# Loads of queries, keys and values from the fifth tile on issued by ScalarE instead of SyncE

## The chip, the cores and the metric

The kernel runs on one NeuronCore of a Trainium2 chip. The metric is the device time of one execution in microseconds (us). The engines are TensorE (PE in the profile; PEld is its loading of weights), VectorE (DVE), ScalarE (ACT), GpSimd (POOL) and SyncE (SP), which here only issues DMAs.

## The reference

Windowed causal attention over 8 batches of 8 heads, 576 positions and 64 columns a head, then one block of a network on the 4608 tokens of 512 columns:

```python
scores = scale * np.matmul(q, k.transpose(0, 1, 3, 2))
mask = (rel >= 0) & (rel < 64)                 # rel: query position less key position
attn = softmax(np.where(mask, scores, -1e9))
x = (attn @ v), heads side by side             # [4608, 512]
h = x @ w_in                                   # [4608, 1024]
solu = h * softmax(h)
ln = (solu - mean) / sqrt(var + 1e-6) * g_ln
out = ln @ w_out                               # [4608, 512]
```

All inputs and the output are float32.

## The kernel before

The 4608 tokens are 36 tiles of 128. One tile goes through these steps, each a function of the kernel:

- `load`: one DMA brings the tile's queries and keys (qk, 640 KB), one the values (v, 512 KB). Each has three buffers, so the load of a tile needs the matmuls of the tile three before it to be done: the scores for qk, `values` for v.
- `scores` and `softmax`: 32 small matmuls (L373) write pS; VectorE takes each head's row maximum (L388, nmx), ScalarE the exponentials (L393, sS and their sums sm), VectorE the reciprocals (L406, L409, rec), and GpSimd scales each head (L411).
- `cross` and `transposes`: the probabilities are transposed. From tile 5 on this is done by DMA: ScalarE copies four heads, split into 16-bit halves, into `raw` (L425), SyncE issues a transposing DMA inside SBUF (L428), and VectorE puts the halves together (L435, PT). Two such rounds make a tile.
- `values`: 32 matmuls (L470) into pO; ScalarE rounds them to xH (L484) and VectorE takes the rest xL (L485).
- `moe_in`: 24 matmuls (L513) into pH, of which there is one buffer, in two halves of 12.
- `moe_norm`: VectorE's maximum over pH (L528), ScalarE's exponential (L530, e), VectorE's product with pH (L533), which is pH's last reader, ScalarE's sum of squares (L539, sq), some short steps (mst), and GpSimd's scaling of e in two halves (L550).
- `moe_cross` and `moe_join`: e is transposed as the probabilities are: VectorE's copy into `raw` (L576), a transposing DMA (L579), VectorE's copy out of it (L589, y), then yH (ScalarE, L593) and yL (VectorE, L595). The first three and the last two tiles use TensorE instead (`moe_transpose`: L610, then yH at L619 and yL at L621).
- `moe_out`: 24 matmuls (L646) into pO, ScalarE's copy to ot (L653), and the store (L654).

Two passes of the weights are split into a rounded part and a rest, hence three matmuls for each pair of blocks. The first tiles use plain float32 matmuls (L502, L634) while the weights (`weight_block`, eight of them through SyncE and `raw`) are still prepared.

The main loop at the end of the kernel calls these functions tile by tile; from tile 6 on (`PAIRS`) two tiles form a group: `group(t)` does the values of tiles t+1 and t+2, the scores, softmax and `cross` of t+3 and t+4, and loads for later tiles. Nothing is issued there. Each call records operations in a `Plan`, with an engine, a cost in ns, what they read and write, and a latency. `Plan.order` then works out due times backwards from TensorE's order and lists all operations by a greedy simulation with those costs; the engines' queues stand in that order and run strictly in it. An operation marked `loose` (all of SyncE's from tile 4 on; `SPL = 3`) may be listed out of the order in which the loop made it. The keys in square brackets are the reads and writes by which the plan orders operations:

```python
plan.dma(P * P * 40, lambda: nc.sync.dma_start(QK(t), qk[t]), [], [("qk", t)],
         t > SPL)
self.op("SP", max(350, size // 340), emit, reads, writes, 2600, loose)
```

Of the kernel before, what the change touches and what calls it, by code (L numbers as in the profile page):

```python
# [18 lines left out]
P = 128  # L19
# [23 lines left out]
PAIRS = 6  # L43

SPL = 3

# [8 lines left out]
class Plan:  # L57
# [12 lines left out]
        self.ops.append((engine, cost, emit, reads, writes, lat + self.LATENCY, loose))  # L70

    def dma(self, size, emit, reads, writes, loose=False):
        self.op("SP", max(350, size // 340), emit, reads, writes, 2600, loose)

    def edges(self):

# [91 lines left out]
def tile_window_attention_solu_moe(  # L168
# [154 lines left out]
    def QK(t):  # L323
        return T("qk", t, [P, NPAIR * (2 * P + WIN)])
# [7 lines left out]
    def V(t, half):  # L332
        return T("v", t, [P, 2, DM])[:, half]

    def load(t, parts=range(2)):

        if 0 in parts:
            plan.dma(P * P * 40, lambda: nc.sync.dma_start(QK(t), qk[t]), [], [("qk", t)],
                     t > SPL)


        if 1 in parts:
            plan.dma(P * P * 32, lambda: nc.sync.dma_start(
                T("v", t, [P, 2, DM]).rearrange("p a n -> p (a n)"), v[t]), [], [("v", t)], t > SPL)

    def SS(t):
        return T("sS", t, [P, H, P])
# [73 lines left out]
    def cross(t):  # L421
        if t < CROSS_P:
            return
        for x in range(2):
            plan.op("ACT", 1050, lambda x=x: nc.scalar.copy(  # L425
                XP(t)[:, x], SS(t)[:, 4 * x:4 * x + 4].bitcast(U16).rearrange("p h (n w) -> p w (h n)", w=2)),
                [("sS", t, 4 * x + i) for i in range(4)], [("raw", NW + 2 * t, x)])
            plan.op("SP", 1250, lambda x=x: nc.sync.dma_start_transpose(  # L428
                XP(t)[:, 2 + x].rearrange("p w (h n) -> p (w h) n", h=4), XP(t)[:, x].rearrange("p w n -> p (w n)")),
                [("raw", NW + 2 * t, x)], [("raw", NW + 2 * t, 2 + x)], 2600, t > SPL)  # L430

# [164 lines left out]
                YL(t)[:, hs], Y(h), YH(t)[:, hs].bitcast(F32)),  # L596
                [("y", t, h), ("yH", t, h)], [("yL", t, h)])

    def moe_transpose(t):
        if crosses(t):  # L600
            moe_join(t)
            return
        for h in range(2):
            def pT(h=h):
                return PE_T(t, h)

            def emit(h=h, pT=pT):
                for f in range(4):
                    c = 4 * h + f
                    nc.tensor.transpose(pT()[:, f], E(t)[:, c * P:(c + 1) * P], ident)  # L610

            hs = slice(4 * h, 4 * h + 4)
            plan.op("PE", 430, emit, [("e", t, h)], [("pS", NTILE + t, h)])
            if t < PLAIN_OUT:
                plan.op("DVE", 620, lambda hs=hs, pT=pT: nc.vector.tensor_tensor(
                    YH(t)[:, hs], pT(), g_sb[:, hs].unsqueeze(2).to_broadcast([P, 4, P]), op=ALU.mult),
                    [("pS", NTILE + t, h), ("g",)], [("yH", t, h)])
                continue
            plan.op("ACT", 560, lambda hs=hs, pT=pT: nc.scalar.copy(YH(t)[:, hs], pT()),  # L619
                    [("pS", NTILE + t, h)], [("yH", t, h)])  # L620
            plan.op("DVE", 620, lambda hs=hs, pT=pT: nc.vector.tensor_sub(  # L621
                YL(t)[:, hs], pT(), YH(t)[:, hs].bitcast(F32)),
                [("pS", NTILE + t, h), ("yH", t, h)], [("yL", t, h)])

    def moe_out(t, middle=None):

        tag = ("pO", t)

        def PO():
            return T(*tag, [P, DM], pool=ps_o)  # L630

        if t < PLAIN_OUT:
            for f in range(NF):
                plan.op("PE", 860, lambda f=f: nc.tensor.matmul(  # L634
                    PO(), YH(t)[:, f], W32(NC + f // 2)[:, f % 2],
                    start=(f == 0), stop=(f == NF - 1)),
                    [("yH", t, f // 4), ("w", NC + f // 2), ("w", NC + f // 2, f % 2)], [tag])
        for f in range(NF if t >= PLAIN_OUT else 0):
            if f == NF // 2 and middle is not None:
                moe_transpose(middle)  # L640
            i, x = NC + f // 2, f % 2
            for k, (y, w, keys) in enumerate((
                    (YH, lambda i, x: WH(i, x), [("yH", t, f // 4), ("H", i, x)]),
                    (YH, lambda i, x: WL(i)[:, x], [("yH", t, f // 4), ("w", NW + i, x)]),
                    (YL, lambda i, x: WH(i, x), [("yL", t, f // 4), ("H", i, x)]))):
                plan.op("PE", 233, lambda f=f, i=i, x=x, k=k, y=y, w=w: nc.tensor.matmul(  # L646
                    PO(), y(t)[:, f], w(i, x), start=(f == k == 0), stop=(f == NF - 1 and k == 2)),
                    keys, [tag])

        def ot():  # L650
            return T("ot", t, [P, DM])

        plan.op("ACT", 580, lambda: nc.scalar.copy(ot(), PO()), [tag], [("ot", t)])  # L653
        plan.dma(P * DM * 4, lambda: nc.sync.dma_start(out[t * P:(t + 1) * P, :], ot()), [("ot", t)], [],  # L654
                 t > SPL)

# [30 lines left out]
    def group(t):  # L687
        on(values, t + 1)
        if t != PAIRS:
            on(values, t + 2)  # L690
        both = t + AHEAD, t + AHEAD + 1
        for u in both:
            on(scores, u)
        for u in (t + AHEAD + 2, t + AHEAD + 3):
            on(load, u, range(1))
        for u in (t + AHEAD + 1, t + AHEAD + 2):
            if u != PAIRS + AHEAD + 2:
                on(load, u, range(1, 2))
        for u in both:
            on(softmax, u)  # L700
            on(cross, u)

    for t in range(NTILE + BEHIND):
        if t < PAIRS:
            on(load, t + AHEAD + 1)
        if t == PAIRS - 1:
            on(load, t + AHEAD + 2, range(1))
        if t == PLAIN_IN:
# [6 lines left out]
        if t < BEHIND:  # L715
            on(moe_in, t, 1)
            on(moe_norm, t)
            on(moe_cross, t)
            on(transposes, t + 1)
            attend(t)  # L720
            on(values, t + 1)
        else:
            even = (t - PAIRS) % 2 == 0
            if t <= PAIRS + 1:
                on(transposes, t + 1)
            elif even:
                on(transposes, t + 1)
                on(transposes, t + 2)
            on(moe_in, t, 1)
            on(moe_norm, t)  # L730
            on(moe_cross, t)
            if t < NTILE:
                on(moe_transpose, t - BEHIND)
            if t < PAIRS:
                on(values, t + 1)
                attend(t)
            elif t == PAIRS + 1:
                on(values, t + 1)
                on(load, t + AHEAD + 1, range(1, 2))
            elif even:  # L740
                group(t)
            if t - BEHIND == PLAIN_OUT:
                for i in range(NC, NC + NF // 2):
                    split(i)

            last = NTILE - 1 <= t < NTILE + BEHIND - 1
            on(moe_out, t - BEHIND, *([t - BEHIND + 1] if last else []))
# [48 lines left out]
```

## Time and profile before

| | us |
|---|---|
| median of three runs | 534.41 (532.65 to 535.96) |
| the profiled execution | 536.71 |
| its span in the profile | 534.9 |
| PE / DVE / ACT / POOL busy | 508.7 / 419.2 / 357.2 / 221.6 |

All rows quoted below come from the profiled execution; their times count from the start of its span. A line of the chain or of the timeline has the start, the length, the engine, the source line and the tiles written and read (`pO<-PT,v`); in square brackets stands how long the engine was idle before and what ended that. SPq is SyncE's queue of DMA issues: a row's length there is the time of issuing, not of the transfer. A row of stretches gives the length, the busy time of each engine with its count, the granted clock of TensorE, the busy share of the DMA engines, and GB/s.

### The profile page before, as it was taken

What the parts mean: (1) busy time and instruction counts of PE and PEld (TensorE: products, weight loads), DVE (VectorE), ACT (ScalarE), POOL (GpSimd) and SP (SyncE); (2) the same over time, 40 slices, a digit from 0 to 9 for tenths busy, and PEclk for the clock granted to TensorE, in tenths of its full rate; (3) what the DMA queues carried; (4) which work ended last, traced back from release to release, by engine and by line L of the source; (5) the groups of instructions that cost most, each with busy time, mean ns of one, the idle gap of its engine ahead of it and who ended that gap; (6) DMA issues with size and microseconds to landing.
All of it is one profiled execution on the core that took longest, in us unless ns stands there. A gap on an engine that the chain in (4) does not pass through costs nothing.

```text
span 534.9 us, 11673 instructions
## 1 busy us (share of the span) xinstructions
PE 508.7 (95%) x4072; PEld 394.4 (74%) x4072; DVE 419.2 (78%) x1327; ACT 357.2 (67%) x959; POOL 221.6 (41%) x406
## 2 busy tenths in 40 slices
PE   2779999999999999999999999979999999999996
PEld 2345576778888887787878787868887888788775
DVE  4979997988787978797979697778777879698630
ACT  4587866679677767677768677684857694956331
POOL 2046067243616461626362526272617161615220
PEclk9989999999999999999999999999999999999999
DMA  8994225789978887777888887967778878457301
GB/s 321 410 387 142 88 74 88 197 191 233 179 217 158 220 155 218 157 217 159 217 158 217 158 217 157 213 132 199 165 156 204 157 215 174 91 104 111 80 21 40
DMA packets 148508, 93.58 MB, mean 175 GB/s; under 512 B 132960, under 2 KB 132960, under 8 KB 148064
## 3 DMA queue, kind: packets, MB, share of 16 engines
q1 hardware_dynamic: 148448, 92.83, 71.0%
q8 instruction: 32, 0.52, 0.4%
q14 instruction: 28, 0.23, 0.1%
HBM read 50.86 MB, written 9.44 MB: 113 GB/s over the span
## 4 chain that ended last, share of the span: by engine, by line
PE 65%; DVE 11%; POOL 8%; DMA 8%; ACT 5%; issue 2%; ACTq 0%; POOLq 0%; DVEq 0%
PE pO L646 26%; PE pH L513 24%; DMA raw<-raw 7%; POOL sS L411 6%; PE pO L470 4%; PE pS L373 4%; PE pH L502 4%; POOL e L550 2%; ACT sS L393 2%; DVE sS L388 1%; DVE raw L576 1%; PE pO L634 1%; DVE PT L435 1%; DVE mst L528 1%; DVE y L589 1%
## 5 line engine op out<-in xcount | busy, mean ns | idle before, releaser
L411 POOL TENSOR_SCALAR sS<-sS,rec 128x128 f32<-128x128 f32 x280 | 122.0, 456 | 49.6 <-DVE nmx L388 26.7
L393 ACT ACTIVATE sS<-sS,nmx 128x128 f32<-128x128 f32 x288 | 111.8, 391 | 10.4 <-DVE nmx L388 9.9
L546 POOL TENSOR_TENSOR mst<-mst,neghalf 128x1 f32<-128x1 f32 x36 | 30.2, 840 | 203.7 <-DVE mst L544 203.7
L646 PE MATMUL pO<-w_outH,yH 128*128 128x512 f32 x272 | 110.1, 405 | 1.2 <-DVE xL L485 1.1
L513 PE MATMUL pH<-w_inH,xH 128*128 128x512 f32 x264 | 106.8, 405 | 3.5 <-DVE mst L533 3.0
L646 PE MATMUL pO<-w,yH 128*128 128x512 f32 x272 | 108.1, 398 | 0.0
L646 PE MATMUL pO<-w_outH,yL 128*128 128x512 f32 x272 | 106.9, 393 | 0.1
L513 PE MATMUL pH<-w,xH 128*128 128x512 f32 x264 | 104.9, 401 | 0.0
L513 PE MATMUL pH<-w_inH,xL 128*128 128x512 f32 x264 | 104.1, 394 | 0.0
L550 POOL TENSOR_SCALAR e<-e,mst 128x512 f32<-128x512 f32 x72 | 66.4, 928 | 45.1 <-DVE mst L547 20.4
L425 ACT COPY raw<-sS 128x1024 uint16<-128x1024 uint16 x62 | 64.3, 1045 | 30.7 <-POOL sS L411 30.6
L589 DVE COPY y<-raw 128x1024 uint16<-128x1024 uint16 x62 | 48.7, 785 | 24.0 <-DMA raw<-raw 23.9
L539 ACT ACTIVATE sq<-e,mst 128x1024 bf16<-128x1024 f32 x36 | 41.4, 1149 | 36.3 <-DVE mst L536 25.0
L513 PEld LDWEIGHTS pH<-w_inH,xH 128*128 128x128 f32 x264 | 49.9, 189 | 18.8 <-issue 3.2
L646 PEld LDWEIGHTS pO<-w_outH,yH 128*128 128x128 f32 x272 | 51.0, 187 | 16.6 <-DVE xL L485 2.4
L576 DVE COPY raw<-e 128x1024 uint16<-128x1024 uint16 x62 | 47.7, 775 | 17.2 <-POOL e L550 17.2
L646 PEld LDWEIGHTS pO<-w_outH,yL 128*128 128x128 f32 x272 | 51.1, 188 | 13.2 <-DVE yL L621 0.5
L513 PEld LDWEIGHTS pH<-w_inH,xL 128*128 128x128 f32 x264 | 50.1, 190 | 12.7 <-issue 0.2
L646 PEld LDWEIGHTS pO<-w,yH 128*128 128x128 f32 x272 | 51.1, 188 | 10.9
L513 PEld LDWEIGHTS pH<-w,xH 128*128 128x128 f32 x264 | 49.9, 189 | 11.4 <-issue 0.2
L388 DVE CUSTOM_DVE_ANT_0 sS<-pS,maskNone 128x128 f32<-128x128 f32 x224 | 53.0, 283 | 4.2 <-PE pS L373 4.2
L593 ACT CAST yH<-y 128x512 fp32r<-128x512 f32 x62 | 38.1, 616 | 26.8 <-DVE y L589 12.5
(66 smaller groups left out, 751.5 us busy)
## 6 DMA issues: line engine op xcount, KB each, us to landing
qk<-qk SPq DMA_DIRECT2D x36, 640.0 KB, 5.6
v<-vS SPq DMA_DIRECT2D x36, 512.0 KB, 4.8
y<-ot SPq DMA_DIRECT2D x36, 256.0 KB, 2.5
raw<-w_out SPq DMA_DIRECT2D x4, 1024.0 KB, 10.8
raw<-w_in SPq DMA_DIRECT2D x3, 1024.0 KB, 11.5
raw<-raw SPq DMA_TRANSPOSE x124, 3.3
raw<-w_in SPq DMA_DIRECT2D x2, 512.0 KB, 6.3
g_sb<-gT SPq DMA_DIRECT2D x1, 4.0 KB, 14.4
```

Source lines behind the costliest of these rows:

```text
L388: plan.op("DVE", 215, lambda h=h: nc.vector.tensor_tensor_reduce(SS(t)[:, h], PS(t)[:, h % 2, h // 2], mk, scale=-SCALE, scalar=BIG, op0=A ...
L393: plan.op("ACT", 390, lambda h=h: nc.scalar.activation(SS(t)[:, h], SS(t)[:, h], AF.Exp, bias=cols("nmx", h), scale=-1.0, accum_out=cols(" ...
L411: plan.op(engine, cost, lambda h=h: v.tensor_scalar(SS(t)[:, h], SS(t)[:, h], rec()[:, h:h + 1], 0.0, ALU.mult, ALU.add), [R], [("sS", t, h)])
L425: plan.op("ACT", 1050, lambda x=x: nc.scalar.copy(XP(t)[:, x], SS(t)[:, 4 * x:4 * x + 4].bitcast(U16).rearrange("p h (n w) -> p w (h n)", ...
L513: plan.op("PE", 233, lambda n=n, c=c, x=x, w=w: nc.tensor.matmul(PH(t)[:, hs], x(t)[:, c], WH(c, h) if w is WH else WL(c)[:, h], start=(n ...
L539: plan.op("ACT", 1200, lambda: nc.scalar.activation(T("sq", t, [P, DFF], BF16), E(t), AF.Square, bias=nmean(), scale=1.0, accum_out=ss()), ...
L546: plan.op("POOL", 560, lambda: nc.gpsimd.tensor_tensor(kk(), kk(), neghalf, op=ALU.pow), [], [key(5)])
L550: plan.op("POOL", 770, lambda h=h, hs=hs: nc.gpsimd.tensor_scalar(E(t)[:, hs], E(t)[:, hs], nmean(), kk(), ALU.add, ALU.mult), [key(4), ke ...
L576: plan.op("DVE", 740, lambda h=h: nc.vector.tensor_copy(EP(t, h), E(t)[:, h * 512:(h + 1) * 512].bitcast(U16).rearrange("p (n w) -> p w n" ...
L589: plan.op("DVE", 740, lambda h=h: nc.vector.tensor_copy(Y(h).bitcast(U16).rearrange("p f (n w) -> p f w n", w=2), TP(t, h).rearrange("p w ...
L593: plan.op("ACT", 620, lambda h=h, hs=hs: nc.scalar.copy(YH(t)[:, hs], Y(h)), [("y", t, h)], [("yH", t, h)])
L646: plan.op("PE", 233, lambda f=f, i=i, x=x, k=k, y=y, w=w: nc.tensor.matmul(PO(), y(t)[:, f], w(i, x), start=(f == k == 0), stop=(f == NF - ...
```

## The change

The loads of tiles 4 to 35 (`t > SPL`) are issued with `nc.scalar` instead of `nc.sync`. For the plan they are operations of ScalarE that cost 70 ns, no longer loose, with an added read, `after`, that puts each behind an operation of ScalarE: behind the last exponential of a tile (`sm`), behind its copy xH, or behind the two copies of probabilities (the new key `gate`). In a group, the first v stands behind xH, the first qk behind the exponentials, and the second of each behind the copies of probabilities of the group's second tile. SyncE's loose operations that are left with `plan.dma`, the stores, cost size // 240 instead of size // 340 in the plan. And where the last two tiles' transposes on TensorE are put inside a `moe_out`, the two halves now stand at a half and at three quarters of it instead of both at a half.

```diff
+RATE = 240
...
-        self.op("SP", max(350, size // 340), emit, reads, writes, 2600, loose)
+        self.op("SP", max(350, size // (RATE if loose else 340)), emit, reads, writes, 2600, loose)
...
-    def load(t, parts=range(2)):
+    def load(t, parts=range(2), after=()):
+
+        queue = nc.scalar if t > SPL else nc.sync
+
+        def dma(size, emit, key):
+            if t > SPL:
+                plan.op("ACT", 70, emit, list(after), [key], 2600 + size // 150)
+            else:
+                plan.dma(size, emit, [], [key])
...
-                [("sS", t, 4 * x + i) for i in range(4)], [("raw", NW + 2 * t, x)])
+                [("sS", t, 4 * x + i) for i in range(4)], [("raw", NW + 2 * t, x), ("gate", t)])
...
-            if f == NF // 2 and middle is not None:
-                moe_transpose(middle)
+            if f in (NF // 2, NF // 4 * 3) and middle is not None:
+                moe_transpose(middle, (f // 2 % 2,))
...
-        for u in (t + AHEAD + 2, t + AHEAD + 3):
-            on(load, u, range(1))
-        for u in (t + AHEAD + 1, t + AHEAD + 2):
-            if u != PAIRS + AHEAD + 2:
-                on(load, u, range(1, 2))
         for u in both:
             on(softmax, u)
             on(cross, u)
+        if t == PAIRS:
+            on(load, t + AHEAD + 2, range(1))
+        on(load, t + AHEAD + 1, range(1, 2), [("xH", t + 1)])
+        on(load, t + AHEAD + 3, range(1), [("sm", t + AHEAD, H - 1)])
+        on(load, t + AHEAD + 4, range(1), [("gate", t + AHEAD + 1)])
+        if t != PAIRS:
+            on(load, t + AHEAD + 2, range(1, 2), [("gate", t + AHEAD + 1)])
...
-            on(load, t + AHEAD + 1)
+            on(load, t + AHEAD + 1, range(1), [("sm", t + 1, H - 1)])
...
+                on(load, t + AHEAD + 1, range(1, 2), [("xH", t + 1)])
                 attend(t)
             elif t == PAIRS + 1:
                 on(values, t + 1)
-                on(load, t + AHEAD + 1, range(1, 2))
+                on(load, t + AHEAD + 1, range(1, 2), [("xH", t + 1)])
```

The new file is longer, so its lines have higher numbers: L428 becomes L436, L579 becomes L587, L610 becomes L618, L393 becomes L401, L530 becomes L538, L425 becomes L433 and L654 becomes L662; the loads are L347 (qk) and L351 (v).

SyncE's queue, in the group that computes the scores of tiles 25 and 26 (t = 22), from the first loads of the group on; before:

```order
L343 DMA v_3930<-vS 128x1024
L343 DMA v_3956<-vS 128x1024
L338 DMA qk_3990<-qk 128x1280
L579 DMA_TRANSPOSE raw_3994<-raw_3994 128x8x128 x2
L338 DMA qk_4035<-qk 128x1280
L579 DMA_TRANSPOSE raw_4087<-raw_4087 128x8x128 x2
L428 DMA_TRANSPOSE raw_4112<-raw_4112 128x8x128
L654 DMA y<-ot_4124 128x512
```

and now:

```order
L587 DMA_TRANSPOSE raw_3972<-raw_3972 128x8x128 x2
L587 DMA_TRANSPOSE raw_4086<-raw_4086 128x8x128 x2
L662 DMA y<-ot_4103 128x512
L436 DMA_TRANSPOSE raw_4116<-raw_4116 128x8x128 x2
L436 DMA_TRANSPOSE raw_4154<-raw_4154 128x8x128 x2
L662 DMA y<-ot_4180 128x512
```

The four loads are gone from SyncE, and the transposes and stores that are left keep their order nearly.

ScalarE's queue in the second half of the same group, from its last exponentials on (sS probabilities, raw their copies, e the exponential over pH, xH the next group's first); before:

```order
L393 ACTIVATE sS_4027,sm_4061<-sS_4027,nmx_4028 128x128 x5
L425 COPY raw_4112<-sS_3961 128x1024
L653 COPY ot_4124<-pO_3987 128x512
L425 COPY raw_4112<-sS_3961 128x1024
L530 ACTIVATE e_4140,mst_4119<-pH_4050,mst_4119 128x1024
L593 CAST yH_4154<-y_4144 128x512
L425 COPY raw_4162<-sS_4027 128x1024 x2
L653 COPY ot_4181<-pO_4117 128x512
L539 ACTIVATE sq_4188,mst_4119<-e_4140,mst_4119 128x1024
L593 CAST yH_4154<-y_4144 128x512
L484 CAST xH_4263<-pO_4224 128x512
```

and now:

```order
L347 DMA qk_4100<-qk 128x1280
L661 COPY ot_4103<-pO_3987 128x512
L433 COPY raw_4116<-sS_3956 128x1024
L538 ACTIVATE e_4131,mst_4119<-pH_4045,mst_4119 128x1024
L433 COPY raw_4116<-sS_3956 128x1024
L433 COPY raw_4154<-sS_4022 128x1024
L601 CAST yH_4162<-y_4144 128x512
L433 COPY raw_4154<-sS_4022 128x1024
L661 COPY ot_4180<-pO_4111 128x512
L547 ACTIVATE sq_4188,mst_4119<-e_4131,mst_4119 128x1024
L601 CAST yH_4162<-y_4144 128x512
L351 DMA v_4202<-vS 128x1024
```

One qk now stands between the exponentials and the copies, and a v, with a qk and then xH behind it, at the end; the exponential over pH has moved ahead of one copy.

TensorE near the end, in the `moe_out` of tile 34 (pO) with the transposes of tile 35 (pS) inside it; before:

```order
L646 MATMUL pO_5941<-w_outH,yL_5924 128x512
L610 MATMUL pS_5963<-ident,e_5901 128x128 x8
L646 MATMUL pO_5941<-w_outH,yH_5918 128x512
L646 MATMUL pO_5941<-w_878,yH_5918 128x512
L646 MATMUL pO_5941<-w_outH,yL_5924 128x512
```

and now:

```order
L618 MATMUL pS_5963<-ident,e_5901 128x128 x4
L654 MATMUL pO_5940<-w_outH,yH_5915 128x512
L654 MATMUL pO_5940<-w_877,yH_5915 128x512
L654 MATMUL pO_5940<-w_outH,yL_5921 128x512
L654 MATMUL pO_5940<-w_outH,yH_5915 128x512
L654 MATMUL pO_5940<-w_877,yH_5915 128x512
L654 MATMUL pO_5940<-w_outH,yL_5921 128x512
L618 MATMUL pS_5963<-ident,e_5901 128x128 x4
```

Four transposes have moved behind six matmuls. Apart from this, the same in the `moe_out` before it, and one half of an early tile's `values`, TensorE's order is unchanged.

More of the change, by code (lines that the diff above doesn't have):

```diff
@@ L333, in V @@
         return T("v", t, [P, 2, DM])[:, half]
-    def load(t, parts=range(2)):
+    def load(t, parts=range(2), after=()):
[5 more added lines that the diff above has]
+                plan.dma(size, emit, [], [key])
         if 0 in parts:
-            plan.dma(P * P * 40, lambda: nc.sync.dma_start(QK(t), qk[t]), [], [("qk", t)],
-                     t > SPL)
+            dma(P * P * 40, lambda: queue.dma_start(QK(t), qk[t]), ("qk", t))
         if 1 in parts:
-            plan.dma(P * P * 32, lambda: nc.sync.dma_start(
-                T("v", t, [P, 2, DM]).rearrange("p a n -> p (a n)"), v[t]), [], [("v", t)], t > SPL)
+            dma(P * P * 32, lambda: queue.dma_start(
+                T("v", t, [P, 2, DM]).rearrange("p a n -> p (a n)"), v[t]), ("v", t))
     def SS(t):
@@ L597, in moe_join, with moe_transpose @@
                 [("y", t, h), ("yH", t, h)], [("yL", t, h)])
-    def moe_transpose(t):
+    def moe_transpose(t, halves=range(2)):
         if crosses(t):
@@ L602, in moe_transpose @@
             return
-        for h in range(2):
+        for h in halves:
             def pT(h=h):
@@ L721, in tile_window_attention_solu_moe @@
             on(values, t + 1)
+            on(load, t + AHEAD + 1, range(1, 2), [("xH", t + 1, 1)])
         else:
```

## The prediction

> **What bounds the kernel now.** I read the shares of the engines first, then the waits of TensorE, then the chain of waits in order of time, to see where a clean stretch differs from a late one.
>
> ```profile
> PE 508.7 (95%) x4072; PEld 394.4 (74%) x4072; DVE 419.2 (78%) x1327; ACT 357.2 (67%) x959; POOL 221.6 (41%) x406
> 145.59 2.02 PE pO L470 x64
> 172.19 2.05 PE pO L470 x64
> 334.17 2.02 PE pO L470 x64
> 365.28 2.02 PE pO L470 x64
> 472.98 2.02 PE pO L470 x64
> ```
>
> TensorE is busy for 95% of the span. From about 145 us on the work comes in groups of two tiles, and each begins with 64 matmuls of line 470. From 145.59 to 172.19 is a clean group: 26.60 us, matmuls end to end. From 172.19 to 472.98 lie eleven groups, 300.79 us; eleven clean ones would be 292.6. So **8.2 us** are lost in this stretch, 4.5 of them in one group (334.17 to 365.28 is 31.11 us). That is all that a change which leaves TensorE's work alone can win here; the loss before 90 us is the start-up, and the end is counted further down. The chain through the worst group names the cause:
>
> ```profile
> 339.57 6.41 DMA raw<-raw
> 346.01 0.76 DVE y L589
> 346.98 2.58 POOL e L550 x2
> 349.55 4.78 POOL sS L411 x8
> 355.31 1.21 ACT e L530 x2
> 356.54 1.23 DVE e L533
> 357.92 7.36 PE pH L513 x24
> ```
>
> A transpose by DMA, issued at 339.57, lands 6.41 us later. VectorE's queue is in order, and its copy out of that transpose (L589) stands at the head, so VectorE stops; GpSimd then gets its column late, its scaling (L411) is late, ScalarE's copy behind it and the exponential (L530) queued behind that copy are late, and pH, of which there is one buffer, comes free late. TensorE waits 2.8 us (the longest below), and then runs at a lower granted clock:
>
> ```profile
> PE pH L513 <- DVE mst L533: 3.0, 2, 2.8
> PE pS L610 <- ACT yH L619: 1.1, 1, 1.1
> 358.00:360.00 2.00, 2.00 (x7) 0.69 0.45 86
> 360.00:362.00 2.00, 2.00 (x6) 0.50 1.05 214
> ```
>
> These are TensorE's waits from 90 us on (total, times, longest), and two stretches of 2 us with the clock in the column before the DMA share. Over the kernel the same wait of VectorE costs 23.9 us in 26 places, mostly absorbed:
>
> ```profile
> DMA to landing us min/median/max: 3.0/3.5/6.9
> DVE y L589 <- DMA raw<-raw: 23.9, 26, 2.0
> 335.29 1.52 SPq L343 DMA_DIRECT2D v<-vS  x2
> 337.27 0.33 SPq L338 DMA_DIRECT2D qk<-qk  x1
> 339.57 3.87 SPq L579 DMA_TRANSPOSE raw<-raw  x2
> 343.53 1.51 SPq L338 DMA_DIRECT2D qk<-qk  x1
> ```
>
> The first row is for the transposes of L579. The typical one lands after 3.5 us; the late one was issued 2.3 to 4.3 us behind two loads of v and one of qk on the one queue there is.
>
> **The loads that move.** The 64 loads of tiles 4 to 35 leave SyncE. They stay as large:
>
> ```profile
> qk<-qk SPq DMA_DIRECT2D x36, 640.0 KB, 5.6
> v<-vS SPq DMA_DIRECT2D x36, 512.0 KB, 4.8
> 324.06 6.06 SPq L428 DMA_TRANSPOSE raw<-raw  x4
> ```
>
> (KB each, median us to landing; then the issue of a group's last transposes of probabilities, the group before the worst one.) Ahead of the first pair of transposes of such a group stood 512 + 512 + 640 = 1664 KB. In the new order one v and one qk are issued before the group begins, behind the previous group's last copy of probabilities. That copy was done when its transpose went out, the last of four (1.28 for its own issue, the median of L428 quoted further down), so by about 324.06 + 6.06 - 1.28 = 328.8, and from there to 339.57 is 10.8 us, more than the 4.8 and 5.6 that the two take; the second qk comes only behind that group's exponentials. One v of 512 KB is left ahead, 31%. I let the loss follow the bytes: 0.31 x 8.2 = 2.5 stays, **5.7 us** goes. The bounds: nothing goes, if the transposes are late for other reasons, and 8.2 goes. I take the value near the upper end because the row of 6.41 against 3.5 has the loads as its only neighbour. In some groups one transpose of L587 now comes right behind the v and qk that are put off, which the old order did not have; that is inside the 2.5.
>
> For TensorE the order of the groups is unchanged. ScalarE's new order helps a little more: the exponential of such a group stands behind one copy of probabilities where two stood. The gain is limited by what is late next: in the same groups VectorE's new order takes the copy of y earlier (behind nine of sixteen score tiles instead of all), so that a landing at 3.5 us is just in time rather than early.
>
> **What ScalarE pays.** Each issue occupies its queue:
>
> ```profile
> L338 SPq DMA_DIRECT2D qk<-qk x36: 328/404/1512, 0.7 to 426.6; - x36
> L343 SPq DMA_DIRECT2D v<-vS x36: 327/340/760, 2.1 to 448.0; - x36
> 255.00:282.00 27.00, 26.86 (x234) 21.60 (x232) 22.69 (x75) 19.05 (x53) 14.48 (x24) 1.00 0.84 186
> ACT xH L484 <- PE pO L470: 31.5, 12, 5.4
> ACT raw L425 <- POOL sS L411: 30.6, 37, 5.0
> ```
>
> On SyncE an issue takes 0.40 (qk) and 0.34 us (v) in the median; before does not show one on ScalarE, so the bounds are 0.33 and 1.51, the ends of qk's row, and I take the medians. 32 x 0.40 + 32 x 0.34 = 24 us, of which 4 x 0.37 = 1.5 us in a group. ScalarE is busy 19.05 of 27 us there, and two of the four stand ahead of the xH copy, for which it waited 31.5 us in 12 places (2.6 each): hidden. The second qk stands ahead of the copies of probabilities and the exponential. The copies waited for GpSimd 30.6 us in 37 places (0.8 each), which hides 0.40 mostly; without that cover the twelve groups that still load would pay 12 x 0.40 = 4.8. I take **1.0 us**, between 0 and 4.8 and nearer 0 because of the 37 waits. A load on ScalarE cannot wait for its buffer there: it stands behind an operation that needed the same matmuls. It can wait for a completion count, of which the program's order shows eight taken in turn, so each load waits for the DMA eight earlier; at 14 DMAs in a group of 26.6 us that one is some 15 us old, against at most 6.9 to land for these transposes.
>
> **The start.** One load stands among the exponentials that the chain runs through:
>
> ```profile
> 29.32 2.42 ACT sS L393 x12
> 32.35 0.63 PE pS L446 x4
> ```
>
> It costs 0.40 there: **0.4 us**, between 0 and 1.5. The last two weight blocks gain a place in SyncE's queue, but the chain here runs through ScalarE. The order of VectorE and ScalarE also shifts a little from 30 to 75 us; nothing prices it, and I allow 1 us either way.
>
> **The end.** The transposes of the last two tiles are cut in halves, six matmuls of L646 apart:
>
> ```profile
> 520.43 0.66 PE L610 MATMUL pS<-ident,e 128*128 128x128 f32 x4
> 522.18 0.63 PE L610 MATMUL pS<-ident,e 128*128 128x128 f32 x4 [1.10 <-ACT yH L619]
> 522.85 0.59 ACT L619 CAST yH<-pS 128x512 fp32r<-128x512 f32 x1 [0.81 <-PE pS L610]
> 523.47 1.29 DVE L621 TENSOR_TENSOR yL<-pS,yH 128x512 fp32r<-128x512 f32 x2 [4.05 <-ACT yH L619]
> ```
>
> The second half waited 1.10 for ScalarE's copy of the first. Six matmuls at 5.63 / 24 = 0.235 us (a block of 24 takes 5.63, shown below) fill 1.4. But the new second half also waits for VectorE's subtraction, one of two in 1.29, so 0.65: about 1.10 + 0.65 - 1.4 = 0.35 remains. For the tile before, whose eight ran without a wait, I charge nothing to 0.35. The end gains **0.7 us**, between 0 and 1.1.
>
> **The sum.** The profiled execution took 536.71 (span 534.9): 536.71 - 5.7 + 1.0 + 0.4 - 0.7 = 531.7. It is 2.3 above the median of the runs, 534.41, and the one stall of 4.5 us need not fall in each. If that 2.3 is part of the 8.2, a median run loses 5.9 and wins 0.69 x 5.9 = 4.1: 534.41 - 4.1 + 1.0 + 0.4 - 0.7 = **531.0**, my forecast.
>
> **Rivals.** *The transposes stay late.* The put-off loads meet other transposes, and all move through the same engines. For it: the DMA share of 0.84 in the row of 255 to 282, so there is little room; SyncE's waits do not name the loads as the cause. Against it: the bytes ahead of the worst ones fall to a third. The time: no gain in the groups, 534.41 + 1.4 - 0.7 = 535.1.
> The Trainium skill, page "DMA: Bandwidth & Descriptors", section "Issuing engines are not separate DMA queues", says that DMAs from ScalarE and SyncE run on the same 16 engines and that issuing from both saves sequencer time alone. By that rule this rival's 535.1 would be the time; the trace of before, with all loads on one queue, neither shows nor denies it. Its section "Queues, rings and completion order" adds that an engine takes packets from its queue rows in turn, by which a transpose would share with a load instead of standing behind it; no run so far shows that.
>
> *All of the loss goes.* Then 534.41 - 5.9 + 0.4 - 0.7 + 0 = 528.2, with ScalarE's issues hidden. For it: the waits of ScalarE above are longer than the issues. Against it: GpSimd and VectorE waits that have no DMA behind them.
>
> *ScalarE is held by SyncE's issues: slower.* The place: v and qk behind the last copy of probabilities, when SyncE issues the transposes of those very copies.
>
> ```profile
> L428 SPq DMA_TRANSPOSE raw<-raw x62: 1231/1275/2242, 80.6 to 491.6; - x62
> 380.63 5.63 PE pO L646 x24
> 391.92 1.23 DVE mst L528
> ```
>
> If each of the two loads has to wait until one transpose is issued, ScalarE stands 2 x 1.28 = 2.6 us longer, with xH and the exponential behind it. The point from which it decides: between two uses of pH TensorE has 24 matmuls of L646, 5.63, to cover the row maximum (1.23), the exponential (1.21) and the product (1.23), 3.67 in all; beyond 1.96 TensorE stands. 2.6 - 1.96 = 0.6 in twelve groups is 7.7, and the gain in the groups is lost: 535.1 + 7.7 = 542.8. For it: on SyncE an issue behind a transpose took up to 1.51. Against it: the 2.6 us of idle time before xH lie just there.
> The Trainium skill's page "Perfetto Trace Analysis", section "DMA Instruction — HWDGE (DVE, Sync)", has the descriptor generator locked for one instruction at a time, shared by the sequencers that use it. By that rule this rival's wait exists; the traces so far, with one issuing queue, cannot show it.
>
> **How the numbers follow.** The forecast (some of the loss goes, 529 to 533) gets 0.50, no gain (535.1) 0.22, all of it gone (528.2) 0.18, ScalarE held (542.8) 0.10. The range 527 to 537 takes in the first three with the unpriced 1 us at the start and the 1.51 of an issue, and leaves out the last and some of the edges. About 1% (5.3 us) is what a measurement can tell from no change: faster than 529.1 has the third case and a little of the first, 0.25; slower than 539.8 the last, 0.10; within 1% the rest, 0.65.
>
> **What would show it.** In the new profile: the transposes of L587 land with a maximum near 4.5 instead of 6.9; VectorE's wait for them falls from 23.9 to about 10; the group that took 31.11 takes about 27; ScalarE issues in 0.33 to 0.5 each and no engine names them as what it waited for; the wait of L618 (now in halves) is about 0.35. A row of issues on ScalarE far over 0.5, or xH waiting for ScalarE's queue, would mean the last rival. I would be wrong altogether if the loss of 8.2 came from GpSimd's own scaling and not from the transposes ahead of it, or if loads on their own queue slow the transposes as much from beside as from ahead.

## The result, and the profile after

| | before | after |
|---|---|---|
| median | 535.10 | **580.59** (576.83 to 585.41) |
| the profiled execution (its span) | 536.71 (534.9) | 577.35 (575.6) |
| ratio of the times | | **1.085** (1.079 to 1.090) |

The forecast was 531.0 with a range to 537: the sign is wrong and the size is 45 us. (Below, runs over 1.5% above the fastest run of the same kernel count in the medians but not in the ratios; `e2` and `e7` have one other run each and so no ratio.)

From the page of the changed kernel: the shares of the engines, the granted clock, the DMA queues, and the chain by engine, first that of before (PE 65%), then the new one.

```profile
PE 519.5 (90%) x4072; PEld 403.5 (70%) x4072; DVE 414.5 (72%) x1327; ACT 357.7 (62%) x959; POOL 216.0 (38%) x406
PEclk9999999999998998999899989998999899999999
q1 hardware_dynamic: 139232, 55.07, 46.2%
q10 hardware_dynamic: 9216, 37.75, 20.7%
PE 65%; DVE 11%; POOL 8%; DMA 8%; ACT 5%; issue 2%; ACTq 0%; POOLq 0%; DVEq 0%
DMA 29%; DVE 18%; PE 18%; POOL 16%; ACT 15%; issue 2%; ACTq 1%; SPq 0%; DVEq 0%; POOLq 0%
```

In the second line PEclk is the granted clock in 40 slices of the span, in tenths. The chain ran mostly over TensorE; now DMA leads it, and all of that 29% is transposes (the line row has `DMA raw<-raw 29%`). TensorE's busy time grew by 10.8 us with the same 4072 instructions; its mean granted clock fell from 0.994 to 0.979 (the slices with an 8), which is 1.5% or some 8 us of that. The other 29.9 of the 40.7 us by which the span grew is idle time. The waits of TensorE and of VectorE from 90 us on (total, times, longest; the third line, L435, is that of before) name that time:

```profile
PE pO L478 <- DVE PT L443: 25.2, 13, 4.7
PE pO L478 <- issue: 4.4, 3, 2.8
DVE PT L435 <- DMA raw<-raw: 1.7, 2, 1.0
DVE PT L443 <- DMA raw<-raw: 43.0, 20, 4.7
DVE y L597 <- DMA raw<-raw: 30.8, 28, 4.8
```

TensorE stands at the `values` of a group (L478, L470 before) for PT, or for nothing that the profile shows ("issue"); 25.2 + 4.4 us is nearly all of the new idle time. VectorE waited 1.7 us in 2 places for the transposes of probabilities before, now 43.0 in 20, and its wait for y did not fall to 10 but rose to 30.8. The landing of the transposes of probabilities before, then the transposes of probabilities (L436) and of e (L587) now, each with the time of issuing (min, median, max, ns) and of landing:

```profile
DMA to landing us min/median/max: 3.0/3.3/5.3
L436 SPq DMA_TRANSPOSE raw<-raw x62: 1231/1287/4564, 76.6 to 530.5; - x62
DMA to landing us min/median/max: 3.0/3.8/8.0
L587 SPq DMA_TRANSPOSE raw<-raw x62: 1231/1260/4028, 87.4 to 541.9; - x62
DMA to landing us min/median/max: 3.0/3.8/10.3
```

One group from its timeline (ACTq are ScalarE's issues, SPq SyncE's, then TensorE's matmuls) and from the chain (the landing of the last transpose, and VectorE's copy out of it):

```profile
294.79 1.23 SPq L436 DMA_TRANSPOSE raw<-raw  x1
294.95 0.35 ACTq L351 DMA_DIRECT2D v<-vS  x1
295.34 0.71 ACTq L347 DMA_DIRECT2D qk<-qk  x1
298.09 4.56 SPq L436 DMA_TRANSPOSE raw<-raw  x1
298.09 6.53 DMA raw<-raw
304.64 0.75 DVE PT L443
302.08 1.62 PE L478 MATMUL pO<-PT,v 128*64 128x64 f32 x48
305.44 0.69 PE L478 MATMUL pO<-PT,v 128*64 128x64 f32 x16 [1.75 <-DVE PT L443]
```

The put-off v and qk go out at 295; the last transpose of the same group's probabilities goes out at 298, 1152 KB behind them, and lands after 6.53 us instead of 3.3. The transpose before it, issued at 294.79, 0.16 us ahead of the v, lands after 6.5 us, too, so loads slow a transpose that they do not stand ahead of. VectorE's copies wait; TensorE does 48 of the group's 64 matmuls and then stands 1.75 us for the last 16, which read the last copy. In the kernel before, the same place of a group looks like this (VectorE's last copy into PT, TensorE's 64 matmuls):

```profile
332.56 0.75 DVE L435 COPY PT<-raw 128x1024 uint16<-128x1024 uint16 x1
334.10 2.08 PE L470 MATMUL pO<-PT,v 128*64 128x64 f32 x64
```

The copy is done at 333.31. The last 16 matmuls, at 0.69 us, begin at about 334.10 + 2.08 - 0.69 = 335.5: a slack of 2.2 us. In the other groups of before it lies between 0.1 and 3.5 us, in the middle at 2.2. A transpose that lands 3.2 us later (6.53 - 3.3) overruns it.

### The profile page after: what moved, and what is told of

The parts are those of the page before. It is cut to its first block, busy times and chain, and to the rows that moved or that the text cites. A ratio compares the mean times of both kernels' runs of the same rounds, so it can differ in the third digit from the quotient of the medians.

```text
span 575.6 us, 11619 instructions
## 1 busy us (share of the span) xinstructions
PE 519.5 (90%) x4072; PEld 403.5 (70%) x4072; DVE 414.5 (72%) x1327; ACT 357.7 (62%) x959; POOL 216.0 (38%) x406
## 4 chain that ended last, share of the span: by engine, by line
DMA 29%; DVE 18%; PE 18%; POOL 16%; ACT 15%; issue 2%; ACTq 1%; SPq 0%; DVEq 0%; POOLq 0%
DMA raw<-raw 29%; POOL sS L419 12%; ACT sS L401 8%; PE pO L654 5%; PE pH L521 4%; POOL e L558 4%; PE pH L510 3%; DVE raw L584 3%; DVE PT L443 3%; DVE mst L536 2%; ACT yH L601 2%; DVE y L597 2%; DVE sS L396 1%; PE pS L381 1%; PE pO L478 1%
## 5 line engine op out<-in xcount | busy, mean ns | idle before, releaser
L419 POOL TENSOR_SCALAR sS<-sS,rec 128x128 f32<-128x128 f32 x280 | 120.7, 450 | 45.4 <-DVE nmx L396 28.8
L401 ACT ACTIVATE sS<-sS,nmx 128x128 f32<-128x128 f32 x288 | 111.9, 391 | 7.8 <-DVE nmx L396 7.8
L554 POOL TENSOR_TENSOR mst<-mst,neghalf 128x1 f32<-128x1 f32 x36 | 22.6, 628 | 247.5 <-DVE mst L552 243.1
L654 PE MATMUL pO<-w_outH,yH 128*128 128x512 f32 x272 | 110.9, 408 | 1.1 <-DVE xL L493 1.1
L654 PE MATMUL pO<-w,yH 128*128 128x512 f32 x272 | 108.5, 399 | 0.0
L654 PE MATMUL pO<-w_outH,yL 128*128 128x512 f32 x272 | 107.1, 394 | 0.4 <-DVE yL L629 0.4
L558 POOL TENSOR_SCALAR e<-e,mst 128x512 f32<-128x512 f32 x72 | 69.6, 973 | 51.6 <-DVE mst L555 28.7
L433 ACT COPY raw<-sS 128x1024 uint16<-128x1024 uint16 x62 | 64.5, 1044 | 26.9 <-POOL sS L419 26.8
L443 DVE COPY PT<-raw 128x1024 uint16<-128x1024 uint16 x62 | 46.0, 752 | 43.2 <-DMA raw<-raw 43.0
L478 PE MATMUL pO<-PT,v 128*64 128x64 f32 x1152 | 45.1, 231 | 31.4 <-DVE PT L443 25.2
L597 DVE COPY y<-raw 128x1024 uint16<-128x1024 uint16 x62 | 48.4, 781 | 31.0 <-DMA raw<-raw 30.8
L538 ACT ACTIVATE e<-pH,mst 128x1024 f32<-128x1024 f32 x36 | 40.1, 1114 | 48.3 <-DVE mst L536 48.2
L478 PEld LDWEIGHTS pO<-PT,v 128*64 128x64 f32 x1152 | 38.9, 142 | 41.8 <-DVE PT L443 27.2
L654 PEld LDWEIGHTS pO<-w_outH,yH 128*128 128x128 f32 x272 | 51.3, 189 | 16.7 <-DVE xL L493 1.6
L654 PEld LDWEIGHTS pO<-w_outH,yL 128*128 128x128 f32 x272 | 51.3, 189 | 13.7 <-DVE yL L629 0.9
L584 DVE COPY raw<-e 128x1024 uint16<-128x1024 uint16 x62 | 45.4, 733 | 20.6 <-POOL e L558 20.5
## 6 DMA issues: line engine op xcount, KB each, us to landing
raw<-w_out SPq DMA_DIRECT2D x4, 1024.0 KB, 10.8
v<-vS SPq DMA_DIRECT2D x4, 512.0 KB, 11.2
```

Source lines behind the costliest of these rows:

```text
L401: plan.op("ACT", 390, lambda h=h: nc.scalar.activation(SS(t)[:, h], SS(t)[:, h], AF.Exp, bias=cols("nmx", h), scale=-1.0, accum_out=cols(" ...
L419: plan.op(engine, cost, lambda h=h: v.tensor_scalar(SS(t)[:, h], SS(t)[:, h], rec()[:, h:h + 1], 0.0, ALU.mult, ALU.add), [R], [("sS", t, h)])
L433: plan.op("ACT", 1050, lambda x=x: nc.scalar.copy(XP(t)[:, x], SS(t)[:, 4 * x:4 * x + 4].bitcast(U16).rearrange("p h (n w) -> p w (h n)", ...
L443: plan.op("DVE", 740, lambda x=x: nc.vector.tensor_copy(PT(t)[:, 4 * x:4 * x + 4].bitcast(U16).rearrange("p h (n w) -> p h w n", w=2), XP( ...
L478: nc.tensor.matmul(PX(t)[r * D:(r + 1) * D, p, ks], V(t, half)[:, h * D:(h + 1) * D], PT(t)[:, h, ks], start=True, stop=True)
L558: plan.op("POOL", 770, lambda h=h, hs=hs: nc.gpsimd.tensor_scalar(E(t)[:, hs], E(t)[:, hs], nmean(), kk(), ALU.add, ALU.mult), [key(4), ke ...
```

## Experiments: one queue or two, and is it the bytes

**`e1`**: after, but all loads on SyncE again, at the places of after.

```diff
-        queue = nc.scalar if t > SPL else nc.sync
+        queue = nc.sync
```

> The changed kernel with one word altered: the 64 loads are issued by SyncE again, in the changed kernel's own order (listed at the places that the plan gave to ScalarE). Three theories of the 45 us. Queue: a load on a second queue runs beside the transposes and stretches them; with one queue again the last transposes of the probabilities land after 3.3 to 5 us wherever they were issued ahead of the loads, and the kernel takes 533 to 545. Place: the loads that are put off come at the wrong moment whatever their queue; it stays at 570 to 585. Order: the loads matter little, the plan's new order on VectorE and ScalarE is what costs; 570 to 585 as well, with the landings short.

579.66 us, ratio to before 1.083 (1.080 to 1.087). The waits are much the same, too, and the transposes of probabilities land late (4.2 us in the median, 8.4 at most), which speaks for "place" and against "order":

```profile
PE pO L478 <- DVE PT L443: 29.7, 7, 6.8
DVE PT L443 <- DMA raw<-raw: 45.9, 21, 6.3
```

So neither the second queue nor ScalarE as the issuer is the cause. The Trainium skill, page "DMA: Bandwidth & Descriptors", section "Issuing engines are not separate DMA queues", says that DMAs run on the same 16 DMA engines and interleave there whichever engine started them; this pair of runs agrees, 580.59 us on two queues and 579.66 on one.

**`e4`**: after, with the order, queue and count of the 64 loads kept, but each bringing 64 KB into a spare buffer; from tile 4 on all tiles compute with tile 3's q, k and v.

```diff
-            dma(P * P * 40, lambda: queue.dma_start(QK(t), qk[t]), ("qk", t))
+            dma(P * P * 40, lambda: queue.dma_start(
+                *((T("qkS", t, [P, P]), qk[t][:, :P]) if t > SPL else (QK(t), qk[t]))), ("qk", t))
```

> The changed kernel with its order kept, but each of the 64 loads brings 64 KB into a spare buffer in place of 512 or 640 KB, and the tiles from the fifth on compute with the fourth tile's queries, keys and values (a part left out: those loads' data). Queue and place: with the bytes gone the transposes land in 3.0 to 4 us, values waits for PT under 5 us in all, 524 to 533. Order: still 565 or more. If issuing on ScalarE were the cost it would stay near 580 too, since the 64 issues are still there.

530.5 us, ratio 0.991 (0.988 to 0.994). VectorE's wait for PT is 8.3 us in 11 places and TensorE's wait for PT 1.6 in 3; the transposes land after 3.3 us or less in the median, though still after up to 5.7 (3 to 4 was expected). With the bytes the whole loss is gone: 64 issues on ScalarE and the new order of all engines are harmless without them.

## Experiments: which part of the change

**`e3`**: before, with the one edit at the tail (the halves at a half and three quarters).

```diff
-            if f == NF // 2 and middle is not None:
-                moe_transpose(middle)
+            if f in (NF // 2, NF // 4 * 3) and middle is not None:
+                moe_transpose(middle, (f // 2 % 2,))
```

> The kernel before with the halves of the last two tiles' transposes at a half and three quarters of a block, and nothing else. By the prediction 0.7 us less than before (0 to 1.1), so 533.5 to 535; all three theories of the 45 us say the same, since none has it here.

535.26 against 535.64 us: 0.999 (0.997 to 1.001), no difference that can be told, and 0.7 us lies within the interval.

**`e2`**: after, with the second pair no longer put off: the second v behind the second xH, the second qk behind the second tile's exponentials.

```diff
-        on(load, t + AHEAD + 4, range(1), [("gate", t + AHEAD + 1)])
+        on(load, t + AHEAD + 4, range(1), [("sm", t + AHEAD + 1, H - 1)])
-            on(load, t + AHEAD + 2, range(1, 2), [("gate", t + AHEAD + 1)])
+            on(load, t + AHEAD + 2, range(1, 2), [("xH", t + 2)])
```

> The changed kernel on ScalarE's queue, but none of the loads is put off behind the copies of probabilities: the second v of a group stands behind the second xH, the second qk behind the second tile's exponentials. Place: the last transposes of the probabilities have no load beside them any more, values no longer waits for PT, 533 to 542. Queue: the transposes of e, which come then, have the loads beside them instead, 545 to 565. Order: 560 or more.

604.68 us (585.84 to 613.98), so no better than after, and over what "place" and "queue" expected. But the loss moved: in the profiled run, one of 608.94 us, VectorE's wait for PT fell to 11.4 us and its wait for y rose to 93.3.

```profile
PE pH L521 <- DVE mst L541: 46.0, 12, 8.4
DVE y L597 <- DMA raw<-raw: 93.3, 29, 9.2
```

Wherever the loads go, the transposes beside them are the late ones; the put-off is not the only bad place. This run alone does not tell the place of the loads from the order that the planner makes of the rest.

**`e6` and `e7`** take these apart. A few lines behind the planner's listing take the loads out of the list and put each behind given operations; every other instruction on every engine keeps its place.

```diff
+    def relocate(self, out):
+        for i, keys in self.moved.items():
+            need = [j for j in range(len(self.ops)) if set(keys) & set(self.ops[j][4])]
...
+            out.remove(i)
+            at = max((out.index(j) for j in need), default=-1) + 1
+            out.insert(at, i)
...
-        return [self.ops[i][2] for i in out]
+        return [self.ops[i][2] for i in self.relocate(out)]
```

`e6` is before's order with the loads at after's places on ScalarE (keys: xH, the eighth `sm`, the second copy of probabilities); `e7` is after's order with the loads on SyncE behind the matmuls that free their buffers. This is near before's place, but not the same: in every second group `e7` issues all four loads (2304 KB) ahead of the first transposes of e, where before issues three at most (1792 KB).

> The order of every instruction but the loads is that of the kernel before; the loads alone are moved, to ScalarE's queue and to the places that the change gives them (behind the copy into xH, behind the eighth exponential, behind the second copy of probabilities). If the order that the planner made for the other instructions is what costs the 45 us, this runs at 533 to 545 us. If the moment at which the loads go out is what costs it, because the put-off v and qk then go beside the last transposes of probabilities, it runs at 565 to 585 us, with VectorE's copies into PT waiting over 30 us for a DMA and the last transpose of a group landing after 6 us or more. Between the two (550 to 560) both count.

> The other half of the same pair: every instruction but the loads in the order of the changed kernel; the loads go back to SyncE and to the moment of the kernel before, right behind the matmuls that free their buffer at the beginning of a group. If the order is what costs, 560 to 585 us, with the waits of VectorE for y grown and those for PT small. If the moment is what costs, 533 to 545 us, with landings of the transposes of probabilities near 3.3 us.

`e6`: 578.74 us, 1.081 (1.075 to 1.086), and VectorE waits for PT 47.4 us in 20 places. The places of the loads alone, in before's order, take 42 of the 45 us. `e7`: 596.06 us (586.32 to 596.97), far outside what "the moment is what costs" expected, but with the signs of "the order is what costs": in the run of 596.97, VectorE's waits for PT are small (6.0) and those for y large (68.4 us). So loads early in the group are no cure in the new order. Whether the order does not bear them, or the fourth load ahead of the transposes of e is what costs, this run does not tell. Of `before`, `after`, `e6` and `e7`, before is the only one without the loss.

**`e5` and `e12`** ask whether the planner could have known.

```diff
 # e5: the two dma_start_transpose operations (that of probabilities is shown)
-                [("raw", NW + 2 * t, x)], [("raw", NW + 2 * t, 2 + x)], 2600, t > SPL)
+                [("raw", NW + 2 * t, x)], [("raw", NW + 2 * t, 2 + x)], 5600, t > SPL)
 # e12: in load
-                plan.op("ACT", 70, emit, list(after), [key], 2600 + size // 150)
+                plan.op("ACT", 70, emit, list(after), [key, ("go", key)], 2600 + size // 150)
+                plan.op("SP", size // RATE, lambda: None, [("go", key)], [("busy", len(plan.ops))], 0, True)
```

> The changed kernel, with the planner told that a DMA transpose takes 3 us longer (5600 where 2600 stood), so that it places the copies out of them and all that follows for a landing of 6 us or so. Loads, queue and rule of place are untouched. If the order is at fault because it counts on landings at 3 us, it comes back to 533 to 548 us although the landings stay late (maximum over 8 us). If the moment of the loads by itself takes the time, it stays at 570 to 585.

> The changed kernel, but the planner is told that a load also fills SyncE's queue for 2.2 us (v) or 2.7 us (qk), so that it doesn't place transposes beside loads as if these took no time. Queue and rule of place are untouched. If the order is wrong because the plan no longer knows of the bytes, most of the loss comes back: 540 to 560 us. If the rule of place alone makes the transposes of probabilities late, it stays at 570 to 585.

`e5`: 565.93 us (560.74 to 570.67), 1.047 (1.042 to 1.051): between its two expectations. With 3 us more allowed for each transpose the wait for PT falls to 32.0 in 12 and the one for y to 6.4 (in the run of 570.67), and by the ratios, 1.047 against 1.085, nearly half of the loss comes back. `e12`: 579.86, 1.085 (1.079 to 1.090): nothing comes back. To tell the plan of the loads as time of SyncE's queue is thus no remedy, while slack for the transposes is one in part.

## Experiments: which of the loads

All four have before's order of everything else; they differ in the loads that go to ScalarE at after's place. "Late" are the twelve v and twelve qk behind the second copy of probabilities.

```diff
+        late = t > 11 and t % 2 == 1
+        queue = nc.scalar if late else nc.sync        # e10: if t > 3 and not late
+        if late and 0 in parts:                       # left out in e13
+            plan.moved[len(plan.ops)] = [("raw", NW + 2 * (t - 3), 1)]
+        if late and 1 in parts:                       # left out in e14
+            plan.moved[len(plan.ops) + (0 in parts)] = [("raw", NW + 2 * (t - 1), 1)]
```

> The order of the kernel before; of a group's four loads only the two that the change puts off furthest (the v and the qk behind the second copy of probabilities) go to ScalarE and to their new place; 24 loads in all, the other 40 stay on SyncE and where they were. If this pair is what makes the last transposes of probabilities late, it takes most of the 43 us of the run that moved all four: 560 to 580 us, VectorE's wait for PT over 30 us. If the loss belongs to the first pair, 533 to 545.

> The complement: the order of the kernel before, the other 40 loads (the v behind the copy into xH, the qk behind the eighth exponential, and those of the tiles ahead of the groups) on ScalarE at their new place, the late pair on SyncE where it was. If the late pair is what costs, 530 to 542 us. If the first pair is, because its qk runs beside the first transposes of probabilities, 555 to 580. If each costs about half, both of these runs lie near 555.

> The order of the kernel before; only the twelve late loads of v (512 KB each) go to ScalarE behind the second copy of probabilities. If the loss follows the bytes, 512 of the pair's 1152 KB, 44% of its 37 us: about 552 us. If the slack ahead of the matmuls on v absorbs the delay by one load, 535 to 541 us.

> The same with the twelve late loads of qk alone (640 KB each). By the bytes, 56% of 37 us: about 557 us. If the slack absorbs one load, 536 to 544 us, a little over the run with v because of the 128 KB more.

| late loads moved | against before, us | ratio | VectorE's wait for PT: us, times |
|---|---|---|---|
| none (before) | | | 1.7, 2 |
| the other 40 loads (`e10`) | 539.34 - 535.87 = +3.5 | 1.006 (1.003 to 1.008) | 2.0, 3 |
| v, 512 KB (`e13`) | 546.76 - 534.48 = +12.3 | 1.021 (1.015 to 1.027) | 22.0, 16 |
| qk, 640 KB (`e14`) | 553.77 - 534.48 = +19.3 | 1.036 (1.030 to 1.042) | 33.0, 19 |
| both, 1152 KB (`e9`) | 573.15 - 535.87 = +37.3 | 1.068 (1.062 to 1.074) | 50.3, 21 |

The waits and landings of `e9`, the late pair alone:

```profile
DVE PT L459 <- DMA raw<-raw: 50.3, 21, 5.1
DVE y L613 <- DMA raw<-raw: 11.2, 13, 2.2
L452 SPq DMA_TRANSPOSE raw<-raw x62: 1231/1287/5342, 79.0 to 529.1; - x62
DMA to landing us min/median/max: 3.0/4.5/9.7
```

The late pair takes 37 of e6's 42 us. It even does to the transposes of e what I had forecast: VectorE's wait for y is 11.2 (my "about 10") against 23.9, and their landing reaches 6.5 at most. What it costs stands in the other row. The loss grows with the bytes: 12.3 and 19.3 us for one load a group, 37.3 for both, which is more than their sum, 31.6; the slack ahead of the matmuls absorbs neither. In twelve groups the pair costs 3.1 us a group. TensorE pays it in `e9` at `values` (L494, 17.6 us under several names) and at `moe_out` (L670, 10.8 us for VectorE's xL, which stands behind the copies into PT in VectorE's queue).

## Experiments: a better place

**`e8`**: before's order, all four loads of a group on SyncE behind its last transpose, qk first, then v. **`e11`**: before, with only the two qk of a group put behind its first two transposes of e. **`e15`**: as `e11`, and the group's second v behind these, too.

```diff
+                plan.moved[len(plan.ops) + n] = [("raw", NW + 2 * (g + 4), 3)] + [("raw", NW + 2 * g + 1, 3)]   # e8
+            plan.moved[len(plan.ops)] = [("raw", NW + 2 * g - 1, 3)]                       # e11: qk
+            plan.moved[len(plan.ops) + (0 in parts)] = [("raw", NW + 2 * t - 11, 3)]       # e15: second v
```

> The order of every instruction but the loads is that of the kernel before, and the loads stay on SyncE; but the four of a group are issued together behind the group's last transpose (of probabilities and of e), when no transpose is under way, and before the next group begins. If what counts is only that no transpose runs beside a load, VectorE's wait for y falls from 23.9 us to under 8, all landings stay under 5 us, and the 8.2 us of loss of the kernel before mostly go: 527 to 531 us. If the four loads last into the next group's first transposes, nothing is won: 534 to 540. If loads so late hold up the scores of the next group, 545 or more.

> The kernel before, order and queue untouched, but the two qk of a group are issued behind its first two transposes of e and so never ahead of them, and before its transposes of probabilities; v stays at the beginning of the group. If a landing is late only by the bytes still on their way when the transpose is issued, the worst landing of e falls from 6.9 us to about 5, VectorE's wait for y from 23.9 to under 15, and 3 to 6 us of the 8.2 us of loss go: 529 to 533 us. If the qk then run into the transposes of probabilities, VectorE's wait for PT rises over 10 us and it is slower than before: 540 to 555.

> The kernel before, order and queue untouched, with both qk behind the group's first two transposes of e, and now the second v of the group behind them too, so that one v of 512 KB stands ahead of these transposes. If the bytes ahead decide, VectorE's wait for y falls from 18 us to under 10 and the time to 528 to 531 us. If three loads in a row then last into the transposes of probabilities (1792 KB, some 8 us, issued about 8 us ahead of them), VectorE's wait for PT rises over 10 us and the time lies at 533 to 545.

`e8`: 592.45 us, 1.105 (1.101 to 1.108). The transposes are nearly on time (VectorE's waits 10.6 for y and 2.1 for PT, landings up to 6.7; under 8 and under 5 were expected), but the loads are not; TensorE's longest wait and a stretch of the chain:

```profile
PE pO L490 <- DMA v<-vS: 41.2, 12, 6.6
204.43 7.31 DMA v<-vS
```

One v of the four is needed at the beginning of the next group, and it stands behind two qk. I expected such a miss at the scores; it came at `values`.

`e11`: **532.14 us, 0.993 (0.990 to 0.996)**, the 3.7 us within the 3 to 6 expected. `e15`: 530.75, 0.992 (0.988 to 0.995), 3.7 us below its own comparison: the second v adds nothing that can be measured, and VectorE's wait for y stays at 19.0 where under 10 was expected. Both beat the two kernels of this case, by 0.7% and 0.8%. The waits of `e11`, the landings of its transposes of e, and its chain where before lost 4.5 us:

```profile
DVE y L608 <- DMA raw<-raw: 18.1, 23, 2.2
DVE PT L454 <- DMA raw<-raw: 2.1, 5, 0.8
DMA to landing us min/median/max: 3.0/3.4/6.5
338.78 4.85 DMA raw<-raw
```

The transpose that landed after 6.41 us (issued at 339.57 before) now takes 4.85, with two v ahead of it and no qk. The wait for y fell less than expected (18.1, not under 15), and the worst landing is still 6.5.

## Why the prediction was wrong, point by point

- **What bounds the kernel: right for the larger part.** Of the 8.2 us, `e11` wins 3.7 by taking qk away from ahead of the transposes, and `e4`, without the bytes, runs 5.1 below its comparison (535.64 - 530.5). That the rest is due to loads is not shown: in `e4` VectorE still waits 12.5 us for y.
- **The loads that move: the step that failed.** I followed the put-off v and qk from the place where they are issued (328.8, behind the copy of probabilities) forward to the next group's transposes, and found them 10.8 us away. I did not ask what else is under way at the place itself: the transposes of those very copies, the row of 324.06 that I had quoted for its end. Behind them VectorE's last copy has 2.2 us of slack in the group shown (0.1 to 3.5 in the others), less than the delay of 3.2. "Inside the 2.5" I had put one transpose of L587 behind the pair; the transpose that counted was L436. By `e9` this costs 37.3 us where the step had a gain of 5.7.
- **What ScalarE pays: right as far as shown.** L347 is issued in 334/348/707 ns (min, median, max), L351 in 334/334/451, and `e4`, with all 64 issues, is faster than before.
- **The start: wrong sign, small.** The `values` ahead of the groups begin at 103.08 where they began at 105.06: 2 us earlier instead of 0.4 later.
- **The end: not contradicted.** Behind the halves of the last two tiles waits of 0.17 and 0.16 us are left (0.35 was forecast for the last); `e3` cannot tell the 0.7 us from nothing.
- **The rivals.** "The transposes stay late" had the cause in a half sentence ("the put-off loads meet other transposes") and priced it at nothing, since I let the loss follow the bytes ahead of the transposes of e alone; a delay counts by the slack of its reader, and these are other transposes with another reader. "ScalarE is held by SyncE's issues" had the place and the sign, but its mechanism is not what costs. In the group shown, v (0.35) and qk (0.71, the longest of all) were issued while SyncE issued the transpose of 294.79 (until 296.02), so at most the 0.36 us by which qk's issue is longer can be such a wait, not 1.28 for each. The section of the Trainium skill on the lock (page "Perfetto Trace Analysis", "DMA Instruction — HWDGE (DVE, Sync)"), by which a wait of this kind exists, gives no length for it; this trace leaves room for 0.36 us. It is SyncE that is held, 4.56 us at 298.09 for one transpose, 2.0 us after ScalarE's two issues were over (295.34 + 0.71 = 296.05).
- **What would show it.** Of my signs the worst landing of L587 (10.3, not 4.5) and the wait for y (30.8, not 10) said "wrong altogether", for the reason given there last: loads slow the transposes as much from beside as from ahead.

What stays open is why the new planner's order does so badly with the loads early in the group (`e7`, 50 us over before in its fastest run): its wait for y shows where, but not how much of it is the order and how much the fourth load ahead of the transposes.

## What to carry to other kernels

When a transfer is moved, list every latency-bound transfer that is under way at its new place, with the slack of the instruction that reads it; a delay beyond that slack is paid in every round of the loop, and here it grew with the bytes, whichever queue they were on. Put bulk loads where no such transfer is due, but count back from their own reader as well: `e8` kept the transposes clean and lost more. This planner knows nothing of shared DMA bandwidth, and `e12` and `e5` show that a few costs in the plan do not make up for it, so move one load at a time and look at the waits behind each.

## What the runs showed of the hardware

With the loads cut to 64 KB (`e4`) a DMA transpose landed after 3.0 us at the least and 3.2 or 3.3 in the median, 5.7 at most. With the full loads at after's places it took up to 8.0 (probabilities) and 10.3 us (e) with them on another queue (after), and up to 8.4 and 6.5 with them on its own (`e1`). For 6 us each, the DMA queues (packets, MB, share of time) with four transposes and a store, in the kernel before from 324 to 330 us, and with v and qk beside three transposes, in the changed one from 296 to 302 us:

```profile
q1 hardware_dynamic: 3731, 1.15, 92.6%
q10 hardware_dynamic: 256, 1.10, 59.8%
q1 hardware_dynamic: 1047, 0.26, 56.2%
```

Without loads, the transposes' queue moved 3731 packets in 6 us (128 of them the store's); beside the loads 1047, while 256 packets of the loads, each about 17 times as large (1.10 MB / 256 against 0.26 MB / 1047), took four fifths of the bytes. And issuing a transpose beside loads can hold the queue: the median is 1.29 us at most, but the longest took 4.56 in the changed kernel and 5.34 in `e9`, against 2.36 in `e4`; in before, with loads on the same queue, it was 4.09.
